# End of attention in another order in a fused attention, soft MoE and squared-ReLU kernel

## The chip, the cores and the metric

One Trainium2 chip; the program runs on one of its cores. The metric is device time in microseconds from start to end of one execution, as a median over runs. All times below are microseconds unless marked ns.

## What is computed

Three layers follow each other, all in fp32 at the interface. Cut to what matters:

```python
# attention: batch 4, 8 heads, 576 positions, head size 64
scores = q @ k.T / 8 + slope[h] * -abs(i - j)      # kept for 0 <= i - j < 128
attn   = softmax(scores)                           # sum + 1e-9
x      = (attn @ v) as (2304, 512)

# soft mixture of experts: 8 experts, 4 slots each, so 32 slots; hidden size 1024
logits = x @ phi                                   # (2304, 32)
d      = softmax over the 2304 tokens              # dispatch
slots  = d.T @ x                                   # (32, 512)
for e in range(8): slot_out[e] = relu(slots[e] @ w1[e]) @ w2[e]
c      = softmax over the 32 slots                 # combine
x      = c @ slot_out

# squared ReLU layer, 2048 wide
out = relu(x @ w_in) ** 2 @ w_out                  # w_in, w_out stored as 64-bit
```

## The kernel before

Work is in units: a unit u is one batch and one pair of heads, 16 in all, four to a batch. Attention runs through blocks of 64 queries; TensorE, VectorE, ScalarE and GpSimd pass score tiles around, and an order for all of them is made at build time by a small planner (`op`, `arrange`), which knows for every step its engine, a guessed cost, what it follows and when it is due. SyncE's transfers are steps of that planner too: the attention inputs z and v, and half tiles of expert weights (`load_half_w`, 512 KB each, 38 of them), each with a time before which it isn't placed (`at=when`). On the chip, `paced` lets such a transfer start only when the VectorE step that stands before it in the order is done.

Each unit ends with xT, its output turned so that features are on partitions. With the four xT of a batch the slot logits are made (`emit_logits`, `emit_logr`, tile L), and `emit_X` turns xT back to tokens on partitions, which `put_x` copies into xn_all. The dispatch softmax runs over all tokens, batch by batch, with a running maximum nm, sum zs and an accumulator acc.

The last unit (u = 15) is not in the planner. The code after `load_extra(2)` is written out by hand in the order in which it stands in each engine's queue, and this is what the change rewrites, lines 651 to 715. It does: the maximum over L and the new nm (L657, L658); the exponentials dT (L659, L660); copies of the logits (L661, L662); `emit_X` and `put_x` of units 14 and 15; copies of the 64 left-over rows to xnr (L676); transposes of dT (L679, L680) and their copies dn and dr (L681, L682); a partition-wide maximum (G, L684); transposes of the logits of the four batches (W, L687) and of the remainder (L692), copied by ScalarE (L690, L696), for the combine softmax; R, dT's product with the tokens, in two halves (L703, L706), each added to acc (L708); ef (L697); X, acc turned into slot inputs (L711), copied to siT (L712). One warm-up matmul (`keep_warm`) ends it.

Then the experts. Sixteen steps `w1_step` (L787; 8 experts by 2 halves of the hidden size) accumulate H from siT and a 1 MB tile of w1 each; sixteen steps of O (L931) follow with w2. Weight tiles wait in a ring of 19 buffers; `wq` is the queue of what is loaded next, `used` counts the buffers, and `pump` issues loads when buffers come free. Five w1 tiles (`extra`, steps 3 to 7) go into memory that attention leaves, and one more into the tile yw, freed last:

```python
wt[wkey("w1", 8)] = yw
sp.dma_start(out=yw, in_=w1[wkey("w1", 8)[1]]...)
```

The tiles f0 to f15 are the last layer's weights, w_in and w_out, 512 KB each, as 64-bit numbers. `conv1` (GpSimd, L840), `conv2` (VectorE, L853 to L857) and `conv3` (ScalarE and GpSimd) turn them into fp32. The last layer starts from so, two small tiles that hold the expert outputs (L959 and the copies behind it), and then runs one long loop of matmuls (L1028), about 216 us of the time.

Of the kernel before, what the change touches and what calls it, by code (L numbers as in the profile page):

```python
# [28 lines left out]
def attn_moe_relu2_kernel(ctx: ExitStack, tc: tile.TileContext, z, v, phi, w1, w2, w_in, w_out, bias, cst, out):  # L29
# [623 lines left out]
    dve.tensor_tensor(out=nm, in0=nm, in1=mx, op=ALU.min)  # L653
    emit_logits(u)
    emit_logr(u)
    L = L_t.pop(b)
    dve.tensor_reduce(out=mx, in_=L[:, 0:192], axis=AX.X, op=ALU.max, negate=True)  # L657
# [9 lines left out]
    X = X_t[u]  # L667
    xt.close()
    load_extra(1)
    six = ctx.enter_context(tc.tile_pool(name="six", bufs=1, side="right"))  # L670
    yw = six.tile([128, 4, 512], F32, name="yw")
    wt[wkey("w1", 8)] = yw
    sp.dma_start(out=yw, in_=w1[wkey("w1", 8)[1]].rearrange("p (a b) -> p a b", a=4))
    put_x(act, u)
    for x, c0 in ((u - 1, 320), (u, 256)):
        dve.tensor_copy(out=xnr[:, sl(x)].rearrange("p (h d) -> p h d", h=2), in_=X[:, :, c0:c0 + 64])  # L676
    act.activation(out=sc, in_=old, func=AF.Exp, bias=nm, scale=-1.0)
    X = bank("S", "X")
    pe.transpose(X[:, 0:128], dT[:, 0:128], ident)  # L679
# [10 lines left out]
    act.activation(out=lgT.rearrange("p (h x) -> p h x", h=2)[:, :, 0:256], in_=W.rearrange("p (h x) -> p h x", h=2), func=AF.Copy)  # L690
    W = bank("B", "W")
    pe.transpose(W[0:64, 0:128], lgR, ident)  # L692
    dve.tensor_reduce(out=s4, in_=dT[:, 0:128], axis=AX.X, op=ALU.add)
    dve.tensor_reduce(out=s6[p], in_=dT[p, 128:256], axis=AX.X, op=ALU.add)
# [89 lines left out]
    def w1_step(i, n, e):  # L784
# [128 lines left out]
    for i in range(8, 16):  # L913
# [4 lines left out]
        if i == 11:  # L918
            conv1(0)
        if i == 13:  # L920
            conv2(0, sp_=0)
# [301 lines left out]
```

## Time and profile before

| | us |
|---|---|
| runs: median of 3 | 388.38 |
| runs: lowest and highest | 387.85, 389.88 |
| profiled execution, its own time | 387.07 |
| its span, first to last instruction | 385.3 |
| TensorE busy in the span | 368.6 (96%) |
| VectorE, ScalarE, GpSimd busy | 282.4, 240.0, 111.0 |
| end of attention to the first expert step | 109.4 to 121.0 |
| expert steps H and O | 121.0 to 153.9 |
| last layer | from about 154 on |

The profile is of one execution. In it PE is TensorE's matmul side, DVE is VectorE, ACT ScalarE, POOL GpSimd, SP SyncE; "L787" is line 787 of the kernel before. The busy time of a matmul holds its pipeline's end, so neighbours overlap. An fp32 matmul shows as two records, a transpose as one. PEclk is the granted share of TensorE's 2.4 GHz.

### The profile page before, as it was taken

How to read it: one execution, taken by the hardware profiler on the slowest of the kernel's cores; microseconds unless marked ns; L12 is line 12 of the kernel's file. 1: busy time of each engine (PE TensorE's matmuls, PEld its weight loads, DVE VectorE, ACT ScalarE, POOL GpSimd, SP SyncE). 2: the span in 40 equal slices, each digit the busy share in tenths (PEclk: the TensorE clock that was granted, in tenths of full speed). 3: DMA queues.
4: the chain of work that ended last, by engine and by line, in shares of the span. 5: the costliest groups of instructions: out<-in, count | busy, mean ns of one | idle time of the engine just before them, and what ended most of it. 6: DMA issues, size and time to landing. Idle time of an engine off the chain costs nothing.

```text
span 385.3 us, 9029 instructions
## 1 busy us (share of the span) xinstructions
PE 368.6 (96%) x3186; PEld 275.9 (72%) x3186; DVE 282.4 (73%) x872; ACT 240.0 (62%) x721; POOL 111.0 (29%) x262
## 2 busy tenths in 40 slices
PE   8989999999769999999999999999999999999996
PEld 6667667576554345877877887888878888888884
DVE  6789899898855655788687888886777774465455
ACT  5899999999841121687677656676667643334440
POOL 5787688866700412041211212111000000000000
PEclk9999999999995999999999999999999999999999
DMA  7799999999999999997003300000000030012004
GB/s 219 250 298 352 368 361 383 385 351 317 283 410 395 347 382 418 418 418 280 3 1 110 111 0 0 2 1 0 3 0 0 17 148 0 3 77 86 3 0 163
DMA packets 20877, 70.90 MB, mean 184 GB/s; under 512 B 2272, under 2 KB 4192, under 8 KB 19168
## 3 DMA queue, kind: packets, MB, share of 16 engines
q1 hardware_dynamic: 20544, 70.07, 48.8%
q8 instruction: 25, 0.41, 0.4%
q10 hardware_dynamic: 288, 0.26, 0.2%
q14 instruction: 20, 0.16, 0.1%
HBM read 65.60 MB, written 4.72 MB: 183 GB/s over the span
## 4 chain that ended last, share of the span: by engine, by line
PE 79%; ACT 11%; DVE 6%; POOL 2%; issue 2%; DVEq 0%; ACTq 0%; POOLq 0%
PE acc L1028 50%; ACT p L211 6%; PE h L984 5%; PE H L787 4%; PE x L310 4%; PE O L931 4%; PE s L191 3%; ACT ptb L291 3%; PE warm L121 2%; PE tp L269 2%; POOL p L244 1%; DVE ptb L293 1%; DVE p L201 1%; PE MX L880 1%; DVE psum L1046 1%
## 5 line engine op out<-in xcount | busy, mean ns | idle before, releaser
L1028 PE MATMUL acc<-whl,arena_gh 128*128 128x512 f32 x864 | 216.5, 394 | 0.0
L1028 PEld LDWEIGHTS acc<-whl,arena_gh 128*128 128x128 f32 x864 | 160.1, 188 | 35.3 <-issue 2.9
L1013 DVE TENSOR_TENSOR arena_gh<-hT,arena_gh 128x384 fp32r<-128x384 f32 (+1 forms) x97 | 53.7, 553 | 29.8 <-ACT arena_gh L1009 24.3
L211 ACT ACTIVATE p<-p,st 128x192 f32<-128x192 f32 (+2 forms) x144 | 61.6, 437 | 6.9 <-DVE st L201 6.6
L996 ACT ACTIVATE acc<-h 128x384 f32<-128x384 f32 x47 | 23.1, 492 | 65.0 <-PE h L984 65.0
L840 POOL TENSOR_SCALAR yw<-f 128x512 f32<-128x512 f32 x32 | 26.9, 847 | 98.8 <-DVE arena_cin L857 53.5
L244 POOL TENSOR_SCALAR p<-p,st 128x128 f32<-128x128 f32 (+1 forms) x142 | 50.0, 366 | 13.5 <-DVE st L221 9.2
L201 DVE CUSTOM_DVE_ANT_0 p<-s,first 128x192 f32<-128x192 f32 (+1 forms) x144 | 40.3, 325 | 3.2 <-PE s L191 3.0
L984 PE MATMUL h<-cst_sb,Mst 128*128 128x384 f32 x95 | 32.2, 339 | 0.1
L236 POOL TENSOR_TENSOR p<-p 128x128 f32<-128x128 f32 (+1 forms) x71 | 28.0, 395 | 12.7 <-ACT p L211 11.2
L310 PE MATMUL x<-ptb,vt 128*64 128x256 f32 (+2 forms) x384 | 31.4, 313 | 0.1
L310 PEld LDWEIGHTS x<-ptb,vt 128*64 128x64 f32 x384 | 22.3, 137 | 9.6 <-ACT ptb L291 1.7
L211 ACT ACTIVATION_READ_ACCUMULATOR p<-p,st 128x1 f32 x144 | 28.7, 199 | 0.0
L1005 DVE TENSOR_TENSOR hT<-acc 128x384 f32<-128x384 f32 x17 | 9.5, 557 | 23.6 <-ACT acc L996 23.6
L1009 ACT ACTIVATE arena_gh<-hT 128x384 fp32r<-128x384 f32 x48 | 24.8, 516 | 0.7
L293 DVE TENSOR_SCALAR ptb<-tp 128x256 f32<-128x256 f32 (+1 forms) x72 | 22.5, 368 | 3.3 <-PE tp L269 3.3
L191 PE MATMUL s<-zq 64*64 64x192 f32 (+2 forms) x396 | 23.7, 324 | 1.0 <-DVE st L201 0.9
L1009 ACT ACTIVATE arena_gh<-acc 128x384 fp32r<-128x384 f32 x47 | 24.2, 516 | 0.6
L996 ACT ACTIVATE hT<-h 128x384 f32<-128x384 f32 x48 | 22.7, 473 | 0.0
L855 DVE SCALAR_TENSOR_TENSOR yw<-f,yw 128x512 int32<-128x512 int32 x32 | 21.9, 689 | 0.8
L984 PEld LDWEIGHTS h<-cst_sb,Mst 128*128 128x128 f32 x95 | 17.8, 188 | 5.3 <-DVE Mst L911 1.3
L871 ACT ACTIVATE whl<-arena_co 128x512 fp32r<-128x512 f32 x16 | 10.1, 630 | 17.5 <-DVE arena_co L857 14.0
(200 smaller groups left out, 455.9 us busy)
## 6 DMA issues: line engine op xcount, KB each, us to landing
w_w<-in_w_dram SPq DMA_DIRECT2D x38, 512.0 KB, 6.5
w_w<-in_w_dram SPq DMA_DIRECT2D x12, 1024.0 KB, 8.9
f<-in_w_in_dram SPq DMA_DIRECT2D x16, 512.0 KB, 9.9
f<-in_w_out_dram SPq DMA_DIRECT2D x16, 512.0 KB, 10.0
zq<-in_z_dram SPq DMA_DIRECT2D x9, 576.0 KB, 5.8
vt<-in_v_dram SPq DMA_DIRECT2D x16, 320.0 KB, 5.9
first<-in_z_dram SPq DMA_DIRECT2D x5, 576.0 KB, 5.8
out_dram<-psum SPq DMA_DIRECT2D x11, 256.0 KB, 2.0
```

Of the source, the lines that this page charges most:

```text
L191: pe.matmul(out=sb_t[2 * w + a][64 * h:64 * h + 64, 256 * i:256 * i + n], lhsT=zbuf(u)[rows, 0, 64 * c:64 * c + 64], rhs=zbuf(u)[rows, 1, ...
L201: x = dve.tensor_tensor_reduce(out=p, in0=sb_t[t][:, 256 * i:256 * i + n], in1=tbl[:, c0 - n:c0], scale=-0.125, scalar=3.0e38, op0=ALU.add ...
L211: act.activation(out=p, in_=p, func=AF.Exp, bias=st[:, k + i:k + i + 1], scale=-1.0, accum_out=st[:, 4 + k + i:5 + k + i])
L236: eng.tensor_tensor(out=ap(True), in0=ap(True), in1=ap(False), op=ALU.subtract)
L244: eng.tensor_scalar(out=p, in0=p, scalar1=st[:, k + i:k + i + 1], scalar2=0.0, op0=ALU.mult, op1=ALU.add)
L310: pe.matmul(out=out, lhsT=v_t[u][:, j, po:po + 64], rhs=queries(u, j, a, b, h), start=(j == 0 or (j == 3 and a == 2)), stop=(j == 4 or (j ...
L840: pool.tensor_scalar(out=y.bitcast(F32), in0=t[:, a, :, 1].bitcast(F32), scalar1=2.0 ** -112, scalar2=0.0, op0=ALU.mult, op1=ALU.add)
L984: pe.matmul(out=hb[-1][:, 0:HB], lhsT=Mst[:, 128 * f:128 * f + 128], rhs=cst_sb[:, c0:c0 + HB], start=True, stop=True)
L996: act.activation(out=rbuf[hf][:, cl], in_=hb[hf][:, cl], func=AF.Relu)
L1009: act.activation(out=lo_t[i][1][hf][:, 0, cl], in_=rbuf[hf][:, cl], func=AF.Square)
L1013: eng.tensor_tensor(out=gh[hf][:, 1, cl], in0=g[hf][:, cl], in1=gh[hf][:, 0, cl].bitcast(F32), op=ALU.subtract)
L1028: pe.matmul(out=acc_t[s], lhsT=gh[:, x, c0:c0 + 128], rhs=w[:, f % 2, y, :], start=(units[i] in firsts and a == 0), stop=(units[i] in last ...
```

## The change

It reorders the end of attention, fills places in TensorE's queue with transposes of the logits, makes the thirteenth w1 tile (`LATE = 12`) the one that goes to yw, lets three w2 tiles pass f1 in the queue of loads, moves the conversion of f0 and f1 to later steps, and has the planner place the half tiles 2250 ns apart.

```diff
-    wq = [wkey("w1", i) for i in range(3)] + [wkey("w1", i) for i in range(9, 16)] + [wkey("w2", i) for i in range(9)]
-    wq += [("f", 0), ("f", 1)] + [wkey("w2", i) for i in range(9, 16)] + [("f", i) for i in range(2, 16)]
+    LATE = 12
+    wq = [wkey("w1", i) for i in range(16) if not 3 <= i < 8 and i != LATE] + [wkey("w2", i) for i in range(9)]
+    wq += [("f", 0)] + [wkey("w2", i) for i in range(9, 12)] + [("f", 1)] + [wkey("w2", i) for i in range(12, 16)] + [("f", i) for i in range(2, 16)]
...
-        when = 15000 + 2400 * min(j, 31) + 1700 * max(0, j - 31)
+        when = 15000 + 2250 * j
...
     dve.tensor_tensor(out=nm, in0=nm, in1=mx, op=ALU.min)
+    emit_X(u - 1)
+    W = bank("S", "W")
+    for bb in range(3):
+        pe.transpose(W[:, 128 * bb:128 * bb + 128], lg(bb), ident)
+    put_x(dve, u - 1)
     emit_logits(u)
     emit_logr(u)
     L = L_t.pop(b)
+    emit_X(u)
+    xt.close()
+    load_extra(1)
...
+    wt[wkey("w1", LATE)] = yw
+    sp.dma_start(out=yw, in_=w1[wkey("w1", LATE)[1]].rearrange("p (a b) -> p a b", a=4))
     dve.tensor_reduce(out=mx, in_=L[:, 0:192], axis=AX.X, op=ALU.max, negate=True)
...
-    emit_X(u - 1)
-    put_x(dve, u - 1)
+    act.activation(out=sc, in_=old, func=AF.Exp, bias=nm, scale=-1.0)
     dve.tensor_scalar(out=bm, in0=blk, scalar1=nm, scalar2=None, op0=ALU.mult)
-    emit_X(u)
...
+    for x, c0 in ((u - 1, 320), (u, 256)):
+        dve.tensor_copy(out=xnr[:, sl(x)].rearrange("p (h d) -> p h d", h=2), in_=X_t[u][:, :, c0:c0 + 64])
     put_x(act, u)
...
     X = bank("S", "X")
+    for _ in range(2):
+        pe.matmul(out=X[:, 256:384], lhsT=ident, rhs=ident, start=True, stop=True)
     pe.transpose(X[:, 0:128], dT[:, 0:128], ident)
...
-    G = bank("S", "G")
+    G = bank("B", "G")
...
-    W = bank("B", "W")
-    for bb in range(4):
-        pe.transpose(W[:, 128 * bb:128 * bb + 128], lg(bb), ident)
...
+    for hf in range(2):
+        emit_R(hf, False)
+        emit_R(hf, True)
+    emit_acc(0)
     dve.tensor_scalar(out=ef, in0=e32, scalar1=gm[:, 0:1], scalar2=None, op0=ALU.mult)
...
+    emit_acc(1)
     X = bank("S", "X")
...
     dve.tensor_copy(out=diag(siT, 4), in_=X[:, 0:128].rearrange("p (a e s) -> p a e s", a=4, e=E))
+    pe.transpose(W[:, 384:512], lg(3), ident)
+    WR = bank("B", "W")
+    pe.transpose(WR[0:64, 0:128], lgR, ident)
+    act.activation(out=lgT.rearrange("p (h x) -> p h x", h=2)[:, :, 0:256], in_=W.rearrange("p (h x) -> p h x", h=2), func=AF.Copy)
...
+    act.activation(out=lgNR, in_=WR[0:64, 0:128], func=AF.Copy)
...
-    keep_warm("S", 1)
...
-        if i in (12, 13, 14):
+        if i > LATE:
             used[0] -= 1
-        elif not 3 <= i < 9:
+        elif not 3 <= i < 8 and i != LATE:
             pump(1, 0)
...
-        if i == 11:
+        if i == 13:
             conv1(0)
-        if i == 13:
+        if i == 15:
+            take_whl(0)
             conv2(0, sp_=0)
-        if i == 14:
-            take_whl(0)
-            conv1(1)
...
-        if i == 0:
-            conv3(0)
         if i == 2:
             emit_hT(1)
+            conv3(0)
         combine_step(16 + i)
-        if i == 4:
+        if i == 5:
+            conv1(1)
+        if i == 8:
             conv2(1)
-        if i == 8:
+        if i == 11:
             conv3(1)
```

`emit_R(hf, rest)` and `emit_acc(hf)` are new names for what stood in the loop over hf: the four matmuls on the tokens or on the rest, and the addition to acc.

TensorE's queue from the last logits to the first half of R, before (xT_105 and xT_106 are units 14 and 15, L the logits, X their transposes, W the transposes of the logits, G the partition-wide maximum, R the slot inputs):

```order
L335 MATMUL L<-xT_106,phi_sb 32x128 x4
L341 MATMUL L<-xT_106,phi_sb 32x64 x4
L347 MATMUL X<-cs,xT_105 128x64 x8
L347 MATMUL X<-cs,xT_106 128x64 x10
L347 MATMUL X<-cs,xT_105 128x64 x2
L679 MATMUL X<-cs,dT 128x128
L680 MATMUL X<-cs,dT 128x128
L684 MATMUL G<-bm,cs 128x4
L687 MATMUL W<-cs,lgT 128x128 x4
L692 MATMUL W<-cs,lgR 64x128
L703 MATMUL R<-xn_all,dn 32x256 x4
L706 MATMUL R<-xnr,phi_sb 32x64 x4
```

and now:

```order
L348 MATMUL X<-cs,xT_105 128x64 x8
L658 MATMUL W<-cs,lgT 128x128 x3
L336 MATMUL L<-xT_106,phi_sb 32x128 x4
L342 MATMUL L<-xT_106,phi_sb 32x64 x4
L348 MATMUL X<-cs,xT_106 128x64 x10
L348 MATMUL X<-cs,xT_105 128x64 x2
L683 MATMUL X<-cs 128x128 x2
L684 MATMUL X<-cs,dT 128x128
L685 MATMUL X<-cs,dT 128x128
L689 MATMUL G<-bm,cs 128x4
L700 MATMUL R<-xn_all,dn 32x256 x4
L697 MATMUL R<-xnr,phi_sb 32x64 x4
```

Unit 14's transposes and three of the four of W now stand ahead of the last logits, and two identity matmuls (L683) ahead of dT's transposes. The fourth of W and the remainder (lgR) have gone behind the slot inputs' L715, as L717 and L719, where the warm-up matmul stood.

VectorE's queue in the same place, from the maximum over L on, before (stat holds maxima and sums, dn and phi_sb the turned dT; the dn row of L697 is ef):

```order
L657 TENSOR_REDUCE stat<-L 128x1
L658 TENSOR_TENSOR stat<-stat 128x1
L428 COPY xn_all<-X 128x2x4x64
L665 TENSOR_SCALAR bm<-cs,stat 128x4
L676 COPY xnr<-X 128x128 x2
L681 COPY dn<-X 128x128
L682 COPY phi_sb<-X 128x128
L688 TENSOR_REDUCE stat<-G 128x1
L693 TENSOR_REDUCE stat<-dT 128x1
L694 TENSOR_REDUCE stat<-dT 32x1
L695 TENSOR_TENSOR stat<-stat 32x1
L697 TENSOR_SCALAR dn<-cs,stat 128x32
```

and now:

```order
L429 COPY xn_all<-X 128x2x4x64
L670 TENSOR_REDUCE stat<-L 128x1
L671 TENSOR_TENSOR stat<-stat 128x1
L677 TENSOR_SCALAR bm<-cs,stat 128x4
L679 COPY xnr<-X 128x128 x2
L686 COPY dn<-X 128x128
L687 COPY phi_sb<-X 128x128
L690 TENSOR_REDUCE stat<-G 128x1
L705 SCALAR_TENSOR_TENSOR acc<-acc,stat,R 128x256
L711 TENSOR_SCALAR dn<-cs,stat 128x32
L705 SCALAR_TENSOR_TENSOR acc<-acc,stat,R 128x256
L716 COPY siT<-X 128x4x8x4
```

The copy into xn_all stands ahead of the maximum over L (L670), ef (L711) between the two additions to acc, and the sums over dT have gone behind siT.

SyncE's queue behind yw, before (f_2424 is f0, f_2452 is f1; w_w are w2 tiles):

```order
L673 DMA yw<-in_w_dram 128x2048
L77 DMA f_2424<-in_w_in_dram 128x1024
L77 DMA f_2424<-in_w_out_dram 128x1024
L77 DMA f_2452<-in_w_in_dram 128x1024
L77 DMA f_2452<-in_w_out_dram 128x1024
L73 DMA w_w_2463<-in_w_dram 128x2048
L73 DMA w_w_2528<-in_w_dram 128x2048
L73 DMA w_w_2541<-in_w_dram 128x2048
L73 DMA w_w_2547<-in_w_dram 128x2048
L73 DMA w_w_2576<-in_w_dram 128x2048
L73 DMA w_w_2589<-in_w_dram 128x2048
L73 DMA w_w_2608<-in_w_dram 128x2048
```

and now (f_2529 is f1):

```order
L669 DMA yw<-in_w_dram 128x2048
L78 DMA f_2424<-in_w_in_dram 128x1024
L78 DMA f_2424<-in_w_out_dram 128x1024
L74 DMA w_w_2452<-in_w_dram 128x2048
L74 DMA w_w_2462<-in_w_dram 128x2048
L74 DMA w_w_2520<-in_w_dram 128x2048
L78 DMA f_2529<-in_w_in_dram 128x1024
L78 DMA f_2529<-in_w_out_dram 128x1024
L74 DMA w_w_2543<-in_w_dram 128x2048
L74 DMA w_w_2549<-in_w_dram 128x2048
L74 DMA w_w_2594<-in_w_dram 128x2048
L74 DMA w_w_2606<-in_w_dram 128x2048
```

f1 is fifth in place of second; f2 follows the last of these rows in both.

## Rows read from the trace of the kernel before

**Rows 1.** The page, part 2: granted TensorE clock in 40 slices, in tenths.

```profile
PEclk9999999999995999999999999999999999999999
```

**Rows 2.** Windows: length, busy us (instructions) of PE, PEld, DVE, ACT, POOL; PEclk, DMA share, GB/s.

```profile
112.00:116.00 4.00, 2.23 (x17) 1.32 (x20) 1.82 (x9) 2.27 (x8) 0.00 (x0) 0.79 1.02 430
...
120.00:124.00 4.00, 3.90 (x20) 1.31 (x19) 3.26 (x16) 0.93 (x3) 0.00 (x0) 0.50 0.94 390
```

**Rows 3.** Chain that ended last, 109 to 126 us: start, us, engine and line.

```profile
110.70 0.37 DVE stat L657
...
111.35 0.42 ACT dT L659
111.77 0.23 ACT dT L660
...
115.36 1.01 PE R L703 x8
116.38 0.26 PE R L706 x8
...
116.66 0.49 DVE acc L708
...
118.49 1.85 PE X L711 x8
...
121.03 3.64 PE H L787 x16
124.67 0.31 PE G L800 x2
```

**Rows 4.** Timeline, same stretch: start, us, instruction, count, [idle before <- releaser].

```profile
111.17 0.68 DVE L428 COPY xn_all<-X 128x512 f32<-128x512 f32 x1
...
112.06 0.33 PE L680 MATMUL X<-cs,dT 128*128 128x128 f32 x1
...
113.12 0.49 DVE L676 COPY xnr<-X 128x128 f32<-128x128 f32 x2 [1.13 <-ACT xn_all L426]
113.53 0.28 DVE L681 COPY dn<-X 128x128 f32<-128x128 f32 x1
...
114.31 0.58 ACT L690 ACTIVATE lgT<-W 128x512 f32<-128x512 f32 x1
114.80 0.24 DVE L697 TENSOR_SCALAR dn<-cs,stat 128x32 f32<-128x32 f32 x1
...
114.94 0.42 PE L692 MATMUL W<-cs,lgR 128*64 128x128 f32 x1 [1.76 <-ACT lgT L690]
...
115.40 0.27 ACT L696 ACTIVATE dT<-W 64x128 f32<-64x128 f32 x1 [0.51 <-PE W L692]
```

**Rows 5.** Line L673 (tile yw): its transfer and time to landing; a window as above.

```profile
L673 SPq DMA_DIRECT2D yw<-in_w_dram x1: 432/432/432, 111.8 to 111.8; - x1
...
DMA to landing us min/median/max: 14.0/14.0/14.0
...
144.00:148.00 4.00, 4.00 (x80) 2.42 (x76) 3.96 (x10) 0.63 (x1) 0.04 (x1) 1.00 1.01 422
```

**Rows 6.** Timeline, 152 to 156 us: f2's conversion and the copy of so.

```profile
152.79 0.69 POOL L840 TENSOR_SCALAR yw<-f 128x512 f32<-128x512 f32 x1 [3.55 <-DMA f<-in_w_in_dram]
...
154.25 0.68 DVE L853 TENSOR_SCALAR yw<-yw 128x512 int32<-128x512 int32 x1
...
155.25 0.42 DVE L428 COPY so<-X 128x256 f32<-128x256 f32 x1 [0.32 <-PE X L959]
```

**Rows 7.** Timeline, PE alone, 99 to 104 us: the idle spell before L347.

```profile
102.36 0.52 PE L347 MATMUL X<-cs,xT 64*128 64x64 f32 x10 [1.35 <-ACT ptb L291]
```

**Rows 8.** Lines L165, the z tile issued at 56.7, and L191, its first use.

```profile
L165 SPq DMA_DIRECT2D first<-in_z_dram x1: 332/332/332, 56.7 to 56.7; - x1
...
DMA to landing us min/median/max: 8.0/8.0/8.0
...
L191 PE MATMUL s<-first x4: 216/217/218, 66.2 to 66.3; 64*64 64x64 f32 x4
```

More of the change, by code (lines that the diff above doesn't have):

```diff
@@ L656, in attn_moe_relu2_kernel @@
     L = L_t.pop(b)
+    emit_X(u)
+    xt.close()
+    load_extra(1)
+    six = ctx.enter_context(tc.tile_pool(name="six", bufs=1, side="right"))
+    yw = six.tile([128, 4, 512], F32, name="yw")
+    wt[wkey("w1", LATE)] = yw
+    sp.dma_start(out=yw, in_=w1[wkey("w1", LATE)[1]].rearrange("p (a b) -> p a b", a=4))
     dve.tensor_reduce(out=mx, in_=L[:, 0:192], axis=AX.X, op=ALU.max, negate=True)
@@ L691, in attn_moe_relu2_kernel @@
[L691 to L694, printed above, removed]
-    dve.tensor_tensor(out=s4[p], in0=s4[p], in1=s6[p], op=ALU.add)
-    act.activation(out=lgNR, in_=W[0:64, 0:128], func=AF.Copy)
-    dve.tensor_scalar(out=ef, in0=e32, scalar1=gm[:, 0:1], scalar2=None, op0=ALU.mult)
-    R2 = pair("R")
-    for hf in range(2):
-        cl = slice(256 * hf, 256 * hf + 256)
-        R = R2[:, hf]
-        for g in range(4):
-            pe.matmul(out=R[32 * g:32 * g + 32, 0:256], lhsT=dn[:, 32 * g:32 * g + 32], rhs=xn_all[:, g, cl], start=True, stop=False,
-                      tile_position=(0, 32 * g), skip_group_check=True)
-        for g in range(4):
-            pe.matmul(out=R[32 * g:32 * g + 32, 64 * g:64 * g + 64], lhsT=dr[:, 32 * g:32 * g + 32], rhs=xnr[:, 256 * hf + 64 * g:256 * hf + 64 * g + 64],
-                      start=False, stop=True, tile_position=(0, 32 * g), skip_group_check=True)
-        dve.scalar_tensor_tensor(out=acc[:, cl], in0=acc[:, cl], scalar=sc, in1=R[:, 0:256], op0=ALU.mult, op1=ALU.add)
+    R2 = pair("R")
@@ new lines, in emit_R @@
+    def emit_R(hf, rest):
+        for g in range(4):
+            if rest:
+                pe.matmul(out=R2[32 * g:32 * g + 32, hf, 64 * g:64 * g + 64], lhsT=dr[:, 32 * g:32 * g + 32], rhs=xnr[:, 256 * hf + 64 * g:256 * hf + 64 * g + 64],
+                          start=False, stop=True, tile_position=(0, 32 * g), skip_group_check=True)
+            else:
+                pe.matmul(out=R2[32 * g:32 * g + 32, hf, 0:256], lhsT=dn[:, 32 * g:32 * g + 32], rhs=xn_all[:, g, 256 * hf:256 * hf + 256], start=True, stop=False,
+                          tile_position=(0, 32 * g), skip_group_check=True)
@@ L709, in attn_moe_relu2_kernel, with emit_acc @@
+    def emit_acc(hf):
+        cl = slice(256 * hf, 256 * hf + 256)
+        dve.scalar_tensor_tensor(out=acc[:, cl], in0=acc[:, cl], scalar=sc, in1=R2[:, hf, 0:256], op0=ALU.mult, op1=ALU.add)
+    for hf in range(2):
+        emit_R(hf, False)
+        emit_R(hf, True)
+    emit_acc(0)
+    dve.tensor_scalar(out=ef, in0=e32, scalar1=gm[:, 0:1], scalar2=None, op0=ALU.mult)
+    emit_acc(1)
     X = bank("S", "X")
@@ L712, in attn_moe_relu2_kernel @@
     dve.tensor_copy(out=diag(siT, 4), in_=X[:, 0:128].rearrange("p (a e s) -> p a e s", a=4, e=E))
+    pe.transpose(W[:, 384:512], lg(3), ident)
+    WR = bank("B", "W")
+    pe.transpose(WR[0:64, 0:128], lgR, ident)
+    act.activation(out=lgT.rearrange("p (h x) -> p h x", h=2)[:, :, 0:256], in_=W.rearrange("p (h x) -> p h x", h=2), func=AF.Copy)
+    dve.tensor_reduce(out=s4, in_=dT[:, 0:128], axis=AX.X, op=ALU.add)
+    dve.tensor_reduce(out=s6[p], in_=dT[p, 128:256], axis=AX.X, op=ALU.add)
+    act.activation(out=lgNR, in_=WR[0:64, 0:128], func=AF.Copy)
+    dve.tensor_tensor(out=s4[p], in0=s4[p], in1=s6[p], op=ALU.add)
     dve.scalar_tensor_tensor(out=zs, in0=zs, scalar=sc, in1=s4, op0=ALU.mult, op1=ALU.add)
     dve.tensor_tensor(out=gm[:, 2:3], in0=gm[:, 0:1], in1=zs, op=ALU.mult)
-    keep_warm("S", 1)
     ps1.close()
```

11 lines of the change are left out of this document (removed).

## The prediction

> **What bounds the kernel now.** I read the page's row of the granted clock first: TensorE runs at its upper level, 2.4 GHz, but for one notch in the first third [rows 1]. The windows of 4 us place it [rows 2]: 0.79 in 112 to 116 us, 0.50 (1.2 GHz) up to 124, with DMA at 390 to 430 GB/s meanwhile. That is the end of attention, the stretch that the change rewrites, so the chain of waits comes next [rows 3], for what followed what between the last logits and the first expert tile, and then the timeline [rows 4], for why TensorE stood. The reader is to see four things. The chain goes through every engine in turn. TensorE's transpose of the logits' remainder (L692) waited 1.76 us for ScalarE's copy L690, and the R matmuls that form slot inputs stood behind it in the queue. VectorE waited 1.13 us with L676 for a ScalarE copy. And after that idling the clock fell, so that R, X and the first two expert steps H ran at half speed: sixteen H records take 3.64 us here.
>
> **Part by part, what the change does to TensorE's path.** Times are on the profiled execution's scale.
>
> *The maximum.* The copy of the last but one unit's transposes into xn_all, 0.68 us (start to start 0.60), now stands ahead of the maximum over L on VectorE. The engine is free some 0.2 before 110.70, where that maximum (L657) starts today, so the loss lies between 0 and 0.6; I take 0.4, and the exponential moves from 111.35 to 111.75. What hides the moved copy today is the wait for the exponential; that cover is given up.
>
> *To the first R.* Two exponentials (0.42, and 0.23 more in the chain) and the second transpose of dT (0.33) end at about 112.8. VectorE's xnr copies no longer stand behind ScalarE's copy, so dn (0.28) follows at once: R begins at 113.15 instead of 115.36 [rows 3, 4]. The three block transposes and X of the last but one unit run before the logits, while ScalarE evicts xT; the last block and the remainder go behind X. The two added identity matmuls cost nothing: they lie in 111.5 to 112.2, where TensorE waits for the exponential. Without that cover they would cost at most twice the 0.33 of a transpose of that size (L680) [rows 4].
>
> *R and X.* In the order shown above nothing stands between the two halves of R. At full clock each is half of 1.08 + 0.26, so both end at 114.5; today the second waits for acc of the first. Then acc (0.49) and ef (0.24) on VectorE, X from 115.2, and half of its 1.85: 116.15. Two transposes follow, and ScalarE's two copies of them (0.58 and 0.27), for which the first H now has to wait, since its accumulator takes their banks: H starts at 117.1. That is **3.9 us** ahead of 121.03.
>
> *The expert steps.* If the clock stays up, the 3.64 us halve (**1.8** gained) and G's 0.31 too (**0.15**). TensorE's own sum is 3.9 + 1.8 + 0.15 = 5.85 us.
>
> *The sums* over dT move behind the slot inputs. They are three short steps on 128 columns, none longer than dn's 0.28, and feed G only after two H steps, 1.8 us later. Nothing is lost.
>
> **What the loads allow.** Tile yw is issued at 111.8 and lands 14.0 us later, at 125.8 [rows 5]. It stands behind the five extra tiles, which are issued at the same places as before, and the queue is full. At 422 GB/s [rows 5] a tile of 1.05 MB takes 2.5 us. Now H step 8 would start at 117.1 + 7.4 + 0.15 = 124.7, so with yw at step 8 it would wait 1.1 us; at step 12 it is due at 128.9 and hidden by 3. Step 7's tile, the one just before yw, lands at 123.3 and is due at 123.7: barely covered.
>
> Next in the queue are f0, seven w2 tiles, f1 in their midst, and the first half of f2, 9.5 tiles or 23.7 us. The slots come free earlier than today, so I expect no hole: f2's half lands at 149.5, where today it lands just before 152.79 [rows 6], because the stream had holes while TensorE was late. It matters for this reason: POOL's scaling of f2 (0.69) releases VectorE's L853 (0.68), and behind that stands the copy of so, at 155.25, without which the second layer can't start. With f2 at 149.5, L853 starts at 150.3 and so at 151.0: a gain of **4.25 us**. TensorE alone would have so at 155.25 - 5.85 = 149.4. The later wins. The last w2 tile, just ahead of f2, lands at 148.3 and is due at 147.1; that wait of 1.2 lies inside the 1.6 by which f2 is late, so it costs nothing more.
>
> The three w2 tiles that pass f1 are the reason why w2 isn't later still. f1 then lands at 125.8 + 5 x 2.5 = 138.3; its two scalings and six VectorE steps of 0.7 end near 144, five before the end of O: hidden. If that cover went, so would move by the rest.
>
> The half tiles. From 15 us on the plan asks for one each 2.25 us instead of 2.4 until the 32nd; then it was 1.7. In SP's order one or two more stand ahead of each attention load. Lower end of the cost: minus 1.6, should the extra tiles enter the queue so much sooner that loads stop binding (then TensorE's 5.85 holds). Upper end: below, as a rival. I take nought, since the extra tiles' issue hangs on attention's end and not on the plan.
>
> **Sum.** 387.07 - 4.25 = 382.8 us against the profiled execution. The runs shown lie above it, the lowest by 0.8, the median by 1.3. I add the 0.8 and not the 1.3, since the stretch at half clock, where runs can differ, is the one that goes: **383.6 us**. Against the median that is 1.2% less; what this measurement can tell from no change is 0.5%, or 1.9 us.
>
> **Rivals.**
>
> *The clock falls anyway.* For it: the new order leaves TensorE short idle spells (0.5 to 0.7 us at 111.5, 0.6 behind R), and part of the filling is transposes. Against it: the longest spell by my sum is 0.7, against 1.76 today; and at 102.36 TensorE had idled 1.35 us in one piece and the clock stayed up, in the slices ahead of the notch [rows 1, 7]. The price: X takes its full 1.85 (0.93 lost), H starts at 118.0, and up to about 124.6, just ahead of G's row, where the low stretch ended, 6.6 us of H run at half speed (3.3 lost). 5.85 - 4.2 leaves 1.6 gained: 385.4, or 386.2 on the runs' scale; a shorter low stretch gives what lies between. The Trainium skill, "TensorE: Matmul & The Clock Gate", section on PE-mode transpose, says that a transpose "doesn't count as PE-busy the same way". By that the filling with logits' transposes would be worth little, and this rival's 386.2 would be the time; no row here separates transposes from other work, and the idle spells shrink whichever work fills them. Chance 0.2.
>
> *The loads don't bind*, and TensorE's own sum holds: 387.07 - 5.85 + 0.8 = 382.0. For it: the half tiles come sooner. Against it: DMA at 390 to 430 GB/s in that stretch [rows 2]. Chance 0.12.
>
> *Crowded attention loads: slower.* The z tile issued at 56.7 landed 8.0 us later, at 64.7, and its first score matmul ran at 66.2 [rows 8]: 1.5 spare, the least of the later z tiles. One more half tile ahead of it costs 1.25 (half of 2.5): just inside. If the queue grew instead by more than 1.5 + 4.25 = 5.75 us, four to five half tiles, attention would end so much later that the change loses; at seven half tiles the time is 383.6 + 8.75 - 1.5 = 390.9. Against it: the order shows one more there, not five. Chance 0.05.
>
> *The change doesn't do what it says*, because f2 stays where it is (holes remain in the stream): so moves by what f2 moves, from 0 to 4.25, say 2: 385.9. Chance 0.08.
>
> **Numbers.** The forecast itself has 0.55: clock up, loads binding, 383.6. Faster by over 0.5% means under 386.4: the forecast, the loads that don't bind, most of the case of the unmoved f2 and half of the clock case, 0.55 + 0.12 + 0.06 + 0.1, less 0.05 for what I haven't seen: 0.78. Slower 0.06, the same 0.16. The range runs from TensorE's sum without the 0.8, 381.2, to just past the clock case, 386.8; it leaves out the crowded loads and what stays below all of it.
>
> **What would show it.** Right: a granted clock of 1.00 from 112 to 128 us; first H near 117.1; sixteen H records in 1.85; no TensorE wait longer than 0.8 before it; R in one piece; f2's half landing near 149.5 and L853 right behind POOL; a short wait of O on a w2 tile. Wrong: a clock under 0.9 in any 4 us before 128; R waiting on xn_all or a first H much past 117.5; score matmuls waiting on z between 55 and 90 us; H step 7 or 12 waiting for its tile; or so following TensorE and not f2.

## The result, and the profile after

The changed kernel takes **384.26 us** (median of 4 executions, 383.6 to 385.66) against 388.12 for the kernel before on the same chip: ratio 0.990, 95% interval 0.985 to 0.994. Run once more beside three other kernels it took 383.61 (6 executions), ratio 0.988, interval 0.985 to 0.991. The forecast was 383.6, range 381.2 to 386.8, faster.

The profiled execution (383.6 us, span 381.8) has these windows at the end of attention, columns as in [rows 2]:

```profile
112.00:116.00 4.00, 2.65 (x40) 1.81 (x40) 2.15 (x9) 2.08 (x7) 0.00 (x0) 1.00 1.02 428
116.00:120.00 4.00, 3.21 (x25) 1.17 (x24) 2.96 (x13) 1.56 (x5) 0.00 (x0) 0.79 1.02 426
120.00:124.00 4.00, 4.00 (x31) 1.30 (x30) 3.61 (x18) 0.52 (x3) 0.00 (x0) 0.79 0.99 408
```

The clock still falls to 0.50 (1.2 GHz), but later, from 118.3 us on, and for a third of the time: a window of 4 us at 0.79 holds 1.7 us at half clock, so two of them make 3.4 us, where [rows 2] belong to some 10. Such a spell at half clock is called a low stretch below. The chain that ended last (start, us, what) shows what followed what:

```profile
111.92 0.42 ACT dT L672
112.34 0.18 ACT dT L673
...
113.47 0.57 PE R L700 x8
114.04 0.11 PE R L697 x8
114.16 0.52 PE R L700 x8
114.67 0.16 PE R L697 x8
...
114.92 0.16 DVE acc L705
...
115.32 0.24 DVE dn L711
...
115.61 1.08 PE X L715 x8
116.68 0.15 PE W L717
...
116.92 0.39 ACT lgT L720
...
117.42 0.27 ACT dT L723
...
117.73 3.14 PE H L798 x16
120.87 0.52 PE G L811 x2
```

R is one piece at full clock, X takes 1.08 us instead of 1.85, and the first H starts at 117.73 instead of 121.03 [rows 3]. The sixteen H records still take 3.14 us, since the clock falls 0.6 us after they begin. The timeline of the same execution, 145 to 156 us, answers to [rows 6]:

```profile
148.98 1.48 POOL L851 TENSOR_SCALAR yw<-f 128x512 f32<-128x512 f32 x2
...
150.83 0.42 DVE L864 TENSOR_SCALAR yw<-yw 128x512 int32<-128x512 int32 x1
151.83 0.42 DVE L429 COPY so<-X 128x256 f32<-128x256 f32 x1 [0.58 <-PE X L969]
```

The copy of so, the gate to the second layer, comes at 151.83 instead of 155.25, and it waits 0.58 us for TensorE's X. The loads do not bind: f2's half landed at 148.50 (issued at 137.7, 10.8 us to landing), its scaling on POOL followed at 148.98 and was over more than a microsecond ahead of L864 (the POOL row holds both halves of f2), and O never waited for a tile.

**A common zero.** What lies ahead of attention's end drifts from execution to execution: the last group of score matmuls (16 records of L191, now L192) starts at 98.94 us in the profile of before, at 99.32 in this one, and at 101.68 in the latest of the runs below. So kernels are compared from that group on. From it to the copy of so it was 155.25 - 98.94 = 56.31 us, and is 151.83 - 99.32 = 52.51: 3.80 gained, of which 0.38 went to the later start here; 3.42 of the 3.47 us between the two profiled executions are there.

### The profile page after: what moved, and what is told of

The parts are those of the page before. It is cut to its first block, busy times and chain, and to the rows that moved or that the text cites. A ratio compares the mean times of both kernels' runs of the same rounds, so it can differ in the third digit from the quotient of the medians.

```text
span 381.8 us, 9033 instructions
## 1 busy us (share of the span) xinstructions
PE 367.0 (96%) x3188; PEld 275.3 (72%) x3188; DVE 282.5 (74%) x872; ACT 239.7 (63%) x721; POOL 111.2 (29%) x262
## 4 chain that ended last, share of the span: by engine, by line
PE 77%; ACT 10%; DVE 7%; issue 2%; POOL 2%; DVEq 0%; ACTq 0%; POOLq 0%
PE acc L1038 51%; ACT p L212 6%; PE h L994 5%; PE H L798 4%; PE O L940 4%; PE x L311 4%; ACT ptb L292 2%; PE s L192 2%; DVE p L202 2%; PE warm L122 2%; DVE ptb L294 1%; POOL p L245 1%; PE tp L270 1%; PE MX L891 1%; DVE psum L1056 1%
## 5 line engine op out<-in xcount | busy, mean ns | idle before, releaser
L237 POOL TENSOR_TENSOR p<-p 128x128 f32<-128x128 f32 (+1 forms) x71 | 28.0, 394 | 12.5 <-ACT p L212 11.2
L311 PE MATMUL x<-ptb,vt 128*64 128x256 f32 (+2 forms) x384 | 31.4, 313 | 0.1
L311 PEld LDWEIGHTS x<-ptb,vt 128*64 128x64 f32 x384 | 22.3, 137 | 9.6 <-ACT ptb L292 1.7
L192 PE MATMUL s<-zq 64*64 64x192 f32 (+2 forms) x396 | 23.9, 324 | 0.7 <-DVE st L202 0.7
```

Of the source, the lines that this page charges most:

```text
L192: pe.matmul(out=sb_t[2 * w + a][64 * h:64 * h + 64, 256 * i:256 * i + n], lhsT=zbuf(u)[rows, 0, 64 * c:64 * c + 64], rhs=zbuf(u)[rows, 1, ...
L237: eng.tensor_tensor(out=ap(True), in0=ap(True), in1=ap(False), op=ALU.subtract)
L311: pe.matmul(out=out, lhsT=v_t[u][:, j, po:po + 64], rhs=queries(u, j, a, b, h), start=(j == 0 or (j == 3 and a == 2)), stop=(j == 4 or (j ...
```

## The experiments

All numbers in one table. "Clock" counts the executions whose mean granted clock was 0.998 or more: profiled executions at that mean show no low stretch ahead of the program's end, those at 0.993 to 0.995 one of 3.4 us. Lower means (0.985 to 0.991) occur in the new order too, two of the changed kernel's four executions among them, at 0.990; none of these was profiled. A mean of 0.990 over 382 us is 7.6 us at half clock, of which, by estimate, 6 to 7 lie ahead of the program's end: the profiled executions have 0 to 1.8 us of it at the end. The kernel before, in 53 executions beside these, never exceeded 0.991. "Low at" is where the profiled execution has its low stretch. The last two columns are from the last group of scores to the copy of so and to the landing of f2's first half, in the profiled execution.

| kernel | median us (n) | ratio to before, 95% | clock | low at | to so | to f2 |
|---|---|---|---|---|---|---|
| before | 388.38 (3) | | | 114 to 125 | 56.31 | 53.77 |
| changed | 384.26 (4) | 0.985 to 0.994 | 0 | 118 to 122 | 52.51 | 49.18 |
| after_again | 383.61 (6) | 0.985 to 0.991 | 1 | none | 50.89 | 49.27 |
| e1_no_ident | 383.16 (6) | 0.984 to 0.992 | 2 | 118 to 122 | 52.70 | 49.26 |
| e2_fill | 382.56 (6) | 0.982 to 0.991 | 4 | 104 to 107 | 52.20 | 50.45 |
| e11_fill_early | 383.09 (5) | 0.983 to 0.989 | 3 | none | 51.09 | 49.35 |
| e5_fill_all | 382.76 (6) | 0.983 to 0.990 | 5 | none | 50.85 | 49.21 |
| e6_fill_transposes | 382.53 (6) | 0.982 to 0.991 | 4 | 91 to 95 | 50.94 | 48.95 |
| e8_rest_only | 387.94 (12) | 0.998 to 1.003 | 0 | 116 to 126 | 56.59 | 52.32 |
| e7_reorder_only | 384.84 (8) | 0.988 to 0.995 | 4 | none | 52.70 | 51.34 |
| e4_late8 | 384.22 (12) | 0.988 to 0.994 | 2 | 118 to 122 | 52.60 | 51.31 |
| e3_spacing | 384.03 (12) | 0.988 to 0.993 | 3 | 104 to 107 | 52.49 | 50.84 |
| e10_best_no_fill | 381.41 (6) | 0.981 to 0.989 | 4 | none | 50.31 | 49.03 |
| e9_best | 381.95 (5) | 0.980 to 0.986 | 5 | none | 50.45 | 49.13 |

### Which part of the change is the gain

**e8_rest_only**: the changed kernel with the old code from the maximum over L to the end of attention (the block shown in the change), its late tile at step 12. The first lines of the edit, against the changed kernel:

```diff
-    emit_X(u - 1)
-    W = bank("S", "W")
-    for bb in range(3):
-        pe.transpose(W[:, 128 * bb:128 * bb + 128], lg(bb), ident)
-    put_x(dve, u - 1)
     emit_logits(u)
     emit_logr(u)
     L = L_t.pop(b)
...
+    emit_X(u - 1)
+    put_x(dve, u - 1)
...
```

> The changed kernel with the end of attention in the old order: late tile at step 12, w2's tiles ahead of f1, the convolution's places and the spacing as changed. Theory A, these parts gain nothing of themselves, since without the reorder TensorE is late for all its loads: the low clock of 10 us and H's start at 121 are back, time within 0.5 us of the kernel before (388.3). Theory B, part of the gain is in the loads: f2 lands earlier than 152.7 by 2 us or more, and the time is 386 to 387.5, if the copy of so was held by f2 in the kernel before.

Measured: 387.94, no gain; H's low clock is back, as the windows show, and VectorE's timeline shows what so waits for:

```profile
116.00:120.00 4.00, 3.42 (x39) 2.25 (x38) 0.96 (x2) 0.27 (x1) 0.00 (x0) 0.53 1.03 428
120.00:124.00 4.00, 3.90 (x19) 1.75 (x21) 2.89 (x14) 0.93 (x3) 0.00 (x0) 0.50 0.92 385
```

```profile
155.31 0.42 DVE L854 TENSOR_SCALAR yw<-yw 128x512 int32<-128x512 int32 x1
156.31 0.42 DVE L429 COPY so<-X 128x256 f32<-128x256 f32 x1 [0.58 <-PE X L959]
```

f2 came 1.5 us sooner than in the kernel before, counted from the scores, and so no sooner. So in the kernel before TensorE, and not f2, set the time: theory A.

**e7_reorder_only**: the kernel before with the new block alone; in it only the late tile's step differs from the change:

```diff
-    wt[wkey("w1", LATE)] = yw
+    wt[wkey("w1", 8)] = yw
...
```

> The kernel before with the new order of the end of attention alone; yw at step 8, f0 and f1 both ahead of w2's second half, the places of the convolution and the spacing of half tiles are those of before. Theory A, the reorder is the gain and the rest protects it: H starts near 118, but step 8 waits for yw or an O step waits for a w2 tile that f1 has pushed back by 2.5 us, and f2 lands later than 148.5: time 384.8 to 386.5. Theory B, the reorder is all of it: time within 0.4 us of the changed kernel's 384.2. Against both: if it stays above 387, the reorder alone isn't the gain.

Measured: 384.84. Its profiled execution shows what the other parts protect, in PE's, POOL's and VectorE's timeline:

```profile
118.53 1.92 PE L797 MATMUL H<-w_w,siT 128*32 128x512 f32 x16 [0.79 <-ACT dT L722]
127.41 1.06 PE L797 MATMUL H<-yw,siT 128*32 128x512 f32 x8 [1.36 <-DMA yw<-in_w_dram]
...
151.32 0.65 POOL L850 TENSOR_SCALAR yw<-f 128x512 f32<-128x512 f32 x1 [4.74 <-DMA f<-in_w_in_dram]
...
152.00 0.43 DVE L863 TENSOR_SCALAR yw<-yw 128x512 int32<-128x512 int32 x1 [0.32 <-POOL yw L850]
...
152.60 0.42 DVE L428 COPY so<-X 128x256 f32<-128x256 f32 x1 [0.17 <-PE X L969]
```

The clock stays up, H's first records take 1.92 us, and the gain is spent again at step 8, which waits 1.36 us for yw; f2 lands two us later than in the changed kernel, and VectorE's L863 waits for it. Theory A. Against after_again, also without a low stretch, the other parts are worth 52.70 - 50.89 = 1.8 us; the reorder alone, the low clock of before included, 56.31 - 52.70 = 3.6. Both are differences of single executions. The medians bear the second out (384.84 against 387.74 beside it) and can't tell the first: the intervals of e7 and the changed kernel overlap. But e7's four executions without a low stretch took 383.26 to 385.08, and the eight of after_again, e1, e3 and e4, 381.76 to 383.91, with medians of 384.5 and 382.9.

**e4_late8**

```diff
-    LATE = 12
+    LATE = 8
```

> The changed kernel with tile yw at expert step 8 as before instead of 12. It landed at 125.09; step 8 of the changed kernel started 124.9 to 125.0 by its trace (H at 117.73, 3.14 for sixteen records, G, then 48 records at half of the low clock's duration). Theory A, as predicted with the loads near their bound: a wait of 0 to 0.6 us at step 8, hidden or not by what follows: time 384.3 to 384.9. Theory B, the place of the late tile doesn't matter for the time now that the clock's low stretch has pushed the steps back: no wait over 0.2 us and the time within 0.3 us of 384.26.

Measured: 384.22, no difference. The sum in this expectation was wrong: step 8 starts at 126.56, not 124.9 (six steps of 0.9 us follow G), so yw, landed at 125.07, is in time by 1.5. But with `LATE = 8` steps 9 to 15 only count slots and load nothing, f2 lands 2.1 us later, and the copy of so now stands right behind L864, which waits 0.39 us for POOL:

```profile
151.39 0.43 DVE L864 TENSOR_SCALAR yw<-yw 128x512 int32<-128x512 int32 x1 [0.39 <-POOL yw L851]
```

Loads and TensorE come out even.

**e3_spacing**

```diff
-        when = 15000 + 2250 * j
+        when = 15000 + 2400 * min(j, 31) + 1700 * max(0, j - 31)
```

> The changed kernel with the half tiles spaced in the plan as before (2400 per half tile up to the 32nd, then 1700). Theory A, the closer spacing has attention loads finish earlier, so that the extra tiles enter an emptier queue (the first landed at 112.0, 1.4 earlier than before) and that is why the loads did not bind: here f2's half lands at 149.5 or later instead of 148.50, the copy of so is released by VectorE's L864, the time is 0.5 to 1.5 us over 384.26. Theory B, the loads have room in either case: f2 within 0.5 us of 148.50, so set by TensorE, the time within 0.4 us of the changed kernel.

Measured: 384.03, no difference in time. As a test of the queue it is clouded: this execution had its low stretch at 104, which held the end of attention back by some 1.6 us while the half tiles drained (yw was issued 14.0 us behind the last scores, 12.4 in the changed kernel). The other traces show what the spacing does. Counted from the last scores, the last half tile landed at 11.0 to 11.2 us in the three profiles with the old spacing (before, e7, e3) and at 8.6 to 9.7 in the eleven with the new one, so the extra tiles, issued at the same places, meet a shorter queue. yw, behind them, took 14.05 us before (111.76 to 125.81) and 13.22 in e8 (112.55 to 125.77), which has the same old order with the new spacing; 14.81 in e7 (112.55 to 127.36) and 13.33 in the changed kernel (111.76 to 125.09), both with the new order. So the closer spacing shortens yw's transfer by 0.8 to 1.5 us; neither pair differs in anything else up to there but which tile is the late one and what loads are queued behind it. Where a low stretch at 104 gives the queue time to drain, little is left of it: 13.58 in e3, and 13.47 in e2 with the new spacing and its low stretch at the same place.

### Why the clock falls, and when

**after_again**: the changed kernel once more.

> The changed kernel itself once more, beside the next three: 384.3 within 0.5, mean clocks of 0.990 to 0.995 in most executions, and where the mean is 0.998 or more the time is 1.5 to 2 us less.

Measured: 383.61; five executions at 0.990 to 0.995, one at 0.998 with 382.46 us. That one was profiled. One of its windows:

```profile
116.00:120.00 4.00, 3.17 (x26) 1.48 (x26) 2.92 (x13) 1.34 (x4) 0.00 (x0) 1.00 1.01 418
```

And from its timeline, the first H and the way to so:

```profile
118.15 1.92 PE L798 MATMUL H<-w_w,siT 128*32 128x512 f32 x16 [0.79 <-ACT dT L723]
...
149.82 0.43 DVE L864 TENSOR_SCALAR yw<-yw 128x512 int32<-128x512 int32 x1
...
150.66 0.42 DVE L429 COPY so<-X 128x256 f32<-128x256 f32 x1 [0.42 <-PE X L969]
```

The same program with the same waits, and the clock does not fall. By this pair the price of the low stretch is 52.51 - 50.89 = 1.6 us. The times of all 36 executions of after_again, e1, e3 and e4 go by their mean clocks too: the eight at 0.998 or more have a median of 382.9 us, the nineteen at 0.993 to 0.996 383.7, the nine at 0.985 to 0.991 386.6. So one low stretch costs 0.8 to 1.6 us, and what happens in the last group, which no profile caught, costs about 3 more.

**e1_no_ident** takes the two identity matmuls out:

```diff
-    for _ in range(2):
-        pe.matmul(out=X[:, 256:384], lhsT=ident, rhs=ident, start=True, stop=True)
```

> The changed kernel without its two identity matmuls (L683). Theory A, TensorE's idle spells between 111 and 118 us let the clock fall, whatever fills them: the spell ahead of the first transpose of dT grows by about 0.4 us, the stretch at 0.50 begins earlier than 118.3 and takes in R or X; H starts at 118 or later, and the time is 0.5 to 2 us over the changed kernel's 384.26. Theory B, these two matmuls lie under a wait and count for nothing: the low stretch stays at 118.3 to 121.7, H starts at 117.7, the time is the changed kernel's within 0.4 us.

Measured: 383.16. PE's wait ahead of the transposes of dT grows from 0.41 to 1.05 us, the low stretch stays where it was, H starts at 117.66. The median is lower than the changed kernel's, by more than the 0.4 expected but less than the intervals can tell. Theory B in kind: these two matmuls show no worth.

**e2_fill** puts three more in each of the two waits behind R and X (the second group writes a free part of R's bank):

```diff
     X = bank("S", "X")
+    for _ in range(3):
+        pe.matmul(out=X[:, 256:384], lhsT=ident, rhs=ident, start=True, stop=True)
     for kk in range(4):
...
     pe.transpose(WR[0:64, 0:128], lgR, ident)
+    for _ in range(3):
+        pe.matmul(out=R2[:, 0, 256:384], lhsT=ident, rhs=ident, start=True, stop=True)
```

> The changed kernel with six more identity matmuls: three between R and X (the wait of 0.82 us there), three between the transpose of lgR and the first H (the wait of 0.79). Theory A, those two spells are what let the clock fall at 118.3: the windows 112 to 124 all show 1.00, the sixteen H records ahead of G take 1.85 us instead of 3.14, and O ends 1.3 us or more earlier. Then two rivals on what follows: if TensorE's own path sets the end, the copy of so comes at about 150.3 instead of 151.83 and the time falls by 1.3 to 1.8 us, to about 382.7; if the loads take over (f2's half landed at 148.50, so can't come before about 150.0), the time falls by no more than 1.8 either, but so is released by VectorE's L864 and not by TensorE. Theory B, the clock hangs on something else (how long X and R run, or the loads' start): the low stretch stays, the time is 384.3 or, where the fill delays X or H, up to 0.4 more.

Measured: 382.56, four of six executions without a low stretch. The profiled one has none at 118, but one right behind the wait of 1.35 us at 102, where PV matmuls (L311) take 2.92 us instead of 1.97. PE's timeline:

```profile
102.53 0.53 PE L348 MATMUL X<-cs,xT 64*128 64x64 f32 x10 [1.35 <-ACT ptb L292]
102.99 2.92 PE L311 MATMUL x<-ptb,vt 128*64 128x256 f32 x24
```

and the same row in the changed kernel's:

```profile
102.99 1.97 PE L311 MATMUL x<-ptb,vt 128*64 128x256 f32 x24
```

The window behind it, in e2:

```profile
104.00:108.00 4.00, 3.58 (x54) 2.87 (x54) 1.64 (x8) 1.81 (x6) 1.66 (x4) 0.60 0.72 256
```

Neither theory as it stood. This is the wait of [rows 7], behind which the clock had stayed up in the profile of before. e3's execution shows the same place.

**e11_fill_early** fills that wait and the one at 105 instead, and none at the end:

```diff
+        if f is emit_T and a in (NS // 2 - 3, NS // 2 - 2):
+            keep_warm("B", 5 if a == NS // 2 - 3 else 2)
```

> The changed kernel with the seven identity matmuls in the waits at 101.2 and 105.3 us alone, none at the end of attention. Theory A, the low stretch of an execution begins behind one of the long waits, at 101 or at 115 to 118: only the second place is left, and the low stretch is still there in most executions, at 118, with a mean clock of 0.993 to 0.996 and the time of the changed kernel within 0.5 us. Theory C, the wait of 1.35 us at 101 is what matters, and the shorter ones of 0.8 only act where it stands before them: the clock stays at 1.00 in most executions, and the median is 1.5 us under the changed kernel's.

Measured: 383.09; three of five executions without a low stretch, the profiled one among them, although the waits of 0.82 and 0.79 us are still there. That leans to theory C, but five executions don't settle it.

**e5_fill_all** has both fills, so both edits above.

> The fills of e2_fill (three identity matmuls each between R and X and ahead of the first H) and two more: five identity matmuls in TensorE's wait at 101.2 to 102.5 us (1.35, for ScalarE's ptb L292), two in the wait at 105.3 (0.66, for VectorE's xT). In e2_fill and e3_spacing the low stretch of 3.4 us came right behind the first of these, at 103, in the changed kernel at 118.3. Theory A, each execution's one low stretch begins behind one of the long waits between 101 and 118, whichever it is: with all filled no window from 100 to 128 us shows less than 1.00, nearly all executions have a mean clock of 0.998 or more, H starts at 117.7, O ends about 1.7 us earlier than in the changed kernel (half of 3.4), and the median is 381.4 to 382.0. The loads then nearly bind: f2's half at 148.5, the copy of so at 150.1 and not earlier. Theory B, the low stretch comes once in an execution whatever the waits are: it moves to a third place, mean clocks stay at 0.994, median 383 to 384.

Measured: five of six executions without a low stretch; all windows from 84 to 128 us at 1.00, and 50.85 us from the scores to so, where 52.51 - 1.7 = 50.81 was expected. The median, 382.76, is above the expected 381.4 to 382.0, and by its interval it can't be told from the changed kernel's. The profiled execution (382.67) reached the last scores at 100.03, 0.7 later than the changed kernel's, ahead of the first fill; whether the others lost their time there too isn't known. The low stretch did not move to a third place: theory A, but for the size.

**e6_fill_transposes** is e5 with a transpose for every added matmul and for the two of the change (these two are shown):

```diff
-        pe.matmul(out=X[:, 256:384], lhsT=ident, rhs=ident, start=True, stop=True)
+        pe.transpose(X[:, 256:384], ident, ident)
```

> As e5_fill_all, but every added identity matmul, the changed kernel's own two among them, is a transpose of the identity of the same size. Theory A, for the clock work is work: mean clocks and the median as in e5_fill_all within 0.002 and 0.5 us. Theory B, transposes don't hold the clock (what the Trainium skill, 'TensorE: Matmul & The Clock Gate', section on PE-mode transpose, says): the low stretch is back at 103 or 118, mean clocks 0.990 to 0.995 as in the changed kernel, and the median is 1 to 2 us over e5_fill_all's.

Measured: 382.53, four of six executions without a low stretch, 50.94 us from the scores to so. The profiled execution has its low stretch elsewhere. PE's timeline and two windows:

```profile
90.33 0.31 PE L342 MATMUL L<-xT,phi_sb 128*32 128x64 f32 x5 [1.88 <-issue]
```

```profile
88.00:92.00 4.00, 2.12 (x64) 1.65 (x56) 1.54 (x10) 2.19 (x10) 2.65 (x8) 0.90 1.01 347
92.00:96.00 4.00, 4.00 (x48) 2.49 (x44) 3.04 (x18) 3.26 (x16) 1.81 (x5) 0.68 0.61 232
```

It follows a wait of 1.88 us in TensorE's queue that nothing in the profile explains ("issue"); in the changed kernel the same place waits 0.69 us. From 96 to 128 us, where the transposes fill, the clock stays at 1.00. They fill less than the matmuls did: waits of 0.66 us at 104.9, 0.69 ahead of dT's transposes, 0.35 ahead of X and 0.46 ahead of H are left, where e5 has 0.22, 0.41 and none. The Trainium skill, "TensorE: Matmul & The Clock Gate", section on PE-mode transpose, says that transposes don't count as busy in the same way; by that e6 should have been 1 to 2 us over e5, and it isn't (382.53 against 382.76). With six executions each a smaller effect stays open.

**Taken together**: of 48 executions of kernels that leave the three long waits (1.35 us at 102, 0.82 ahead of X, 0.79 ahead of H) unfilled (changed, after_again, e1, e3, e4, e7), 12 had no low stretch; of 28 of those with fills in some or all of them (e2, e5, e6, e9, e11), 21. Among kernels that ran beside each other it is the same: 7 of 30 without (e1, e3, e4) against 4 of 6 with fills (e2); 4 of 8 (e7) against 9 of 12 (e5, e6); 1 of 6 (after_again) against 8 of 10 (e9, e11). That is the evidence for the fills: by the intervals of the medians none of e2, e5, e6 and e11 can be told from the changed kernel. A long wait makes a fall possible, not certain, and which of them it strikes differs between executions.

### A better version, and where the loads bind

**e9_best**: both fills, fewer at the end, and the block drawn together: sums, ef, transposes and ScalarE's copies stand right behind R. The edit against e5; the lines that it takes out behind X (the two transposes, their copies, the sums and the last three fills) are not shown:

```diff
         emit_R(hf, True)
-    emit_acc(0)
+    dve.tensor_reduce(out=s4, in_=dT[:, 0:128], axis=AX.X, op=ALU.add)
...
     dve.tensor_scalar(out=ef, in0=e32, scalar1=gm[:, 0:1], scalar2=None, op0=ALU.mult)
-    emit_acc(1)
+    pe.transpose(W[:, 384:512], lg(3), ident)
+    WR = bank("B", "W")
+    pe.transpose(WR[0:64, 0:128], lgR, ident)
...
+    act.activation(out=lgNR, in_=WR[0:64, 0:128], func=AF.Copy)
     X = bank("S", "X")
-    for _ in range(3):
+    for _ in range(1):
         pe.matmul(out=X[:, 256:384], lhsT=ident, rhs=ident, start=True, stop=True)
+    emit_acc(0)
+    emit_acc(1)
     for kk in range(4):
...
+    for _ in range(2):
+        pe.matmul(out=R2[:, 0, 256:384], lhsT=ident, rhs=ident, start=True, stop=True)
```

> The changed kernel with both fills, and the end of attention drawn together once more: ef, the sums over dT, the last two transposes of the logits and ScalarE's two copies of them stand between R and acc, so that the first H waits for the copy of siT alone. By TensorE's sum: X starts 0.2 earlier (ef no longer between the two acc), H 0.7 to 0.95 earlier than in the changed kernel, counted from X of the last unit, and no low stretch: 1.7 + 0.9 = 2.6 us. By the loads: f2's half lands as in the changed kernel (148.5 on its scale), the copy of so can't come before about 149.7, where the changed kernel had 151.83: 2.1 us. So the loads take over at the last: 2.1 us less than the changed kernel, 382.1 by its median of 384.26, VectorE's L864 waiting for POOL and the copy of so right behind it. If instead the loads come earlier too, as the new X frees slots sooner, up to 2.6: 381.7.

**e10_best_no_fill** is the same without any of the fills; one of the three places is shown:

```diff
-    for _ in range(2):
-        pe.matmul(out=R2[:, 0, 256:384], lhsT=ident, rhs=ident, start=True, stop=True)
```

> As e9_best without the added identity matmuls. H still starts 0.7 to 0.95 earlier than in the changed kernel. Theory A (long waits let the clock fall): the waits behind R and X shrink to 0.3 to 0.5 us, so no low stretch at 115 to 121, but one at 103 in some executions: mean clocks 0.994 to 1.0, median 0.8 to 1.8 us under the changed kernel's. Theory B (fills alone hold the clock): low stretch at 118 as before, median 0.7 to 0.9 under it.

Measured: e9 381.95 us, all five executions between 381.41 and 382.03 and all without a low stretch; ratio 0.983, interval 0.980 to 0.986, so it beats the kernel before by 1.7%. The changed one beside it (0.988, 0.985 to 0.991) is about 0.4% slower: the two intervals touch, but the slowest of e9's five executions, 382.03, lies below the fastest of after_again's six, 382.46. H starts 117.72 - 112.55 = 5.17 us behind the exponential, where it was 117.73 - 111.92 = 5.81: 0.64 sooner, just under the 0.7 to 0.95 expected. And now the loads bind, as VectorE's and POOL's timeline of e9 shows:

```profile
148.99 0.66 POOL L857 TENSOR_SCALAR yw<-f 128x512 f32<-128x512 f32 x1 [1.55 <-DMA f<-in_w_in_dram]
149.68 0.43 DVE L870 TENSOR_SCALAR yw<-yw 128x512 int32<-128x512 int32 x1 [0.36 <-POOL yw L857]
...
150.23 0.42 DVE L429 COPY so<-X 128x256 f32<-128x256 f32 x1
```

f2, POOL, VectorE, so: one behind the other, with no wait for TensorE. The gain, 52.51 - 50.45 = 2.06 us, is the 2.1 that the loads allow and not TensorE's 2.6. e10 has the same picture (L864 waits 0.40 us for POOL) and 50.31; its median is 381.41, but two of six executions had a low stretch, at 384.43 and 385.15. That leans to its theory A, though where the clock fell in those two wasn't profiled, and the median is 2.2 us under after_again's, more than either theory had. The waits ahead of X and H are 0.23 and 0.53 us there. The two kernels can't be told apart by their medians; e9 is the steadier.

## Why the prediction was right, and where it was not

The time was right to 0.7 us, and the reorder did what was said of it. But two steps failed, with opposite signs, and what set the end was not what the prediction named: it had the loads set it at full clock, and TensorE set it with a low clock. Neither the forecast's case nor one of the rivals came, but parts of two of them at once (the clock falls, the loads don't bind). That the number is this near is luck. Counted from the exponential (predicted at 111.75, measured at 111.92 in the changed kernel, 112.35 in after_again):

| step | predicted | changed | after_again |
|---|---|---|---|
| R starts | 1.40 | 1.55 | |
| R ends | 2.75 | 2.91 | |
| X starts | 3.45 | 3.69 | 3.68 |
| H starts | 5.35 | 5.81 | 5.80 |
| f2's half lands | 37.75 | 36.58 | 36.69 |
| copy of so | 39.25 (37.65 by TensorE alone) | 39.91 | 38.31 |

- **The maximum**: the copy ahead of it was to cost 0.4 us. From the scores to the exponential it was 111.35 - 98.94 = 12.41 us and is 111.92 - 99.32 = 12.60: 0.2, inside the bounds.
- **R, X and H**: right in kind. H is 0.46 later than the sum: 0.16 in R (G, ahead of it, waited for ScalarE's lgR), 0.08 up to X, 0.12 in X, 0.10 in ScalarE's two copies.
- **"If the clock stays up"** failed in nine of ten executions of the changed kernel, and the sixteen H records took 3.14 us, not 1.85. The step that failed is the argument against the first rival: "at 102.36 TensorE had idled 1.35 us in one piece and the clock stayed up". That was one execution. In e2 and e3 the clock falls right behind that very wait. The rival's own price, 386.2, supposed 6.6 us of H at half clock; 3.4 came in the profiled execution, so its time lies between, as the rival's last words allow. Two of the other three, at a mean clock of 0.990, took 384.77 and 385.66: by the estimate above they had 6 to 7 us at half clock, near the rival's case and its price.
- **TensorE's own sum**: where the clock did stay up (after_again), so came 0.66 later than the sum, of which 0.46 is H's start and 0.15 the gain on G that did not come (G still takes 0.3 us). The sum was 5.85 us; from the scores to so, 56.31 - 50.89 = 5.42 came.
- **"The later wins"** failed: f2's half came 1.1 us sooner than said, and so waited for TensorE. The term at fault is yw's landing, 14.0 us after its issue: it took 13.3 (13.6 in after_again), and counted from the exponential it landed 0.9 us sooner (13.17 for 14.05; 0.6 in after_again). "I take nought" for the half tiles was the place: the extra tiles' issue does hang on attention's end, but the queue that they enter is shorter (the last half tile lands 8.8 us behind the last scores, for 11.0 before). What happened is part of the lower end that was named there, 1.6. From f2's landing to so it takes 150.23 - 148.91 = 1.3 us where the loads bind (e9), and not 1.5: VectorE's L853 was counted with its 0.68 of before, and the step takes 0.43 there.
- **The loads as a cap** was nonetheless the right way to think: at step 8, yw made H wait 1.36 us (e7; predicted 1.1), and e4, e7, e9 and e10 all show VectorE waiting for POOL's scaling of f2 just ahead of so. In after_again TensorE is only 0.42 us behind that cap.
- **The number** came out near because the misses nearly cancel: 39.91 for 39.25 in the table, a low stretch of 1.6 us and 0.66 in the sum on TensorE's side, and a cap that lay more than 1 us lower than thought. The range spans both rivals' cases and would have held with either.
- **f1 behind w2, and the sums moved**: hidden, as said. O waits for nothing, where a wait of 1.2 us on the last w2 tile was expected, since the tiles came sooner and TensorE later.
- **Crowded attention loads**: nothing of it. The last scores came at 99.05 to 100.03 us in the ten profiles with the new spacing that have no low stretch ahead of them, and at 98.94 to 99.90 in the three with the old one: a spread between executions, with no shift.

What stays open: why the same wait drops the clock in one execution and not in the next; whether the early or the late fill does more; what the executions at 0.985 to 0.991 look like; what the wait marked "issue" in e6 was.

## What to carry to other kernels

A wait behind which the clock held in one profile is no proof that it holds: look at the mean clock of all executions before counting on a full clock, and price the low stretch at its measured length. Where two chains meet (here TensorE's and the loads'), work out both to the same gate, and say how far apart they are; with 0.4 us between them a small miss changes which one sets the end, and the next saving on one side alone is cut off there. The parts of a change that gain nothing alone (e8) can still be what keeps the gain of another (e7: 1.8 us between two profiled executions at full clock).

## What was not expected of the hardware

The low stretch struck at 91, 104 or 118 us in different executions and kernels, each time at or behind one of the long waits, and not at all in others of the same program. And TensorE's queue stood for 1.88 us at L342 in one execution and for 0.69 in another, with nothing in the profile to wait for.
